# Sixty-four small DRAM-to-DRAM copies, spread one by one through the transfer queue of a windowed-attention and two-MLP kernel

## The chip, the cores and the metric

One core of one Trainium2 chip. The metric is the device time of one execution in microseconds (us); "before" is the median of three executions of the same program. One execution was profiled, and its trace is what all rows below come from. TensorE is PE in the rows (PEld is its load of stationary operands), VectorE is DVE, ScalarE is ACT, GpSimd is POOL, and SP is the engine whose queue issues every transfer of this kernel.

## The reference

Attention over a window of 64 keys, then two MLPs, all in float32; some weights arrive as float64 and are read as 64-bit words.

```
B, H, S, D = 4, 8, 576, 64
scores = q @ k^T / sqrt(D), kept where 0 <= i - j < 64, else -1e9
attn   = exp(scores - max); attn = attn / (sum + 1e-9)
x      = attn @ v, as (2304, 512)
h      = x @ w_in;   x = max(0.01 * h, h) @ w_out        # 512 -> 2048 -> 512
h      = x @ w_in2;  out = (max(h, 0) + log1p(exp(-|h|))) @ w_out2
```

## The kernel before

**Tiles and chunks.** The 2304 tokens are 18 attention tiles of 128, six chunks of 384 for the first MLP. A first-MLP step (c, j) is a *product* (`gemm1_p`, letter G, 12 matmuls of 384 columns into a PSUM tile `ph`), an ACT activation `g` (`gemm1_a`, letter P, line 634), a rounded copy `gh` (letter Q, line 640), the remainder `gl` on DVE (letter R, line 646), and the second product (`gemm2`, letter H, 12 matmuls into four PSUM tiles `o`). Two PSUM buffers hold `ph`, so a new G waits until the P of the second last G has been read.

**The order.** Everything up to about 130 us stands in `HEAD`, a list written out by hand: a letter and a number for each piece, one after another. `ordered` chains the pieces on each engine, so that each engine's order is the list's. After `HEAD` a loop over `steps` does the rest, two slots to a step; what attention needs is put into slots by `attention_slots`.

**The weights of the first MLP.** 32 blocks of 512 KB, keyed by j and by 0 (w_in) or 1 (w_out); the text calls them 9_1, 10_0 and so on. Letter l loads one (`load_w`, lines 147 and 152) into one of three buffers `wraw`; a and b narrow it (ACT line 161, then DVE lines 166 and 168), c and d split it into two halves (ACT or DVE line 466, DVE line 246). A load needs the buffer of the load three before it, which is free when that block's line 168 has read it. The numbers behind l, a, b, c, d in `HEAD` are 2j for j_0 and 2j + 1 for j_1.

**Queries and keys by blocks.** Tiles 0 to 5 are turned on PE. From tile 6 on DVE turns them in 32 by 32 blocks, for which q and k must lie block by block in DRAM: `lay_out(b, parts)` copies batch b of q and k there in 32 small copies (line 405, runs of 128 bytes). Batch 1 takes 32 copies of 48 KB, batch 2 takes 32 of 72 KB. `load_blocks` (line 418) then loads one tile's q and k blocks, `tile_u` (lines 893 and 894) turns them on DVE. All copies and loads stand in SP's one queue, in program order.

Before the change the copies are issued four at a time, ahead of a G:

```python
relay = {5 + n: (lay_out, first, range(n * PARTS // 8, (n + 1) * PARTS // 8)) for n in range(8)}
relay |= {14 + n: (lay_out, first + 1, range(n * PARTS // 8, (n + 1) * PARTS // 8)) for n in range(8)}
```

where the number is the count of G's begun, and three G's can follow each other closely in the list.

**The attention results of tile t** go out to DRAM (`cross`, line 933, `turned`) and come back in four copies (`back`, line 937) before PE multiplies them with v (line 913).

Of the kernel before, what the change touches and what calls it, by code (L numbers as in the profile page):

```python
# [21 lines left out]
def tile_window_attention_two_mlps(  # L22
# [75 lines left out]
    PARTS = 2 * NP * (P // TB)  # L98
# [177 lines left out]
    def keep_places():  # L276


        kept["64"] = [sb.tile([P, DM], I64, tag="raw64", bufs=3, name=f"kept64_{n}") for n in range(3)]

    def keep_more():
        kept["cv"] = cv.rearrange("p n x -> p (n x)")
        part = sb.tile([P, 3, DM], F32, tag="part", bufs=1, name="kept_part")
        kept["part"] = part.rearrange("p n x -> p (n x)")
        kept["hi"] = [[kept[nm][:, 2 * DM :] for nm in ("part", "cv")]]
# [3 lines left out]
    def keep_last():  # L289
        kept["hi"].append([pair[:, n].rearrange("p a b -> p (a b)") for n in range(2)])  # L290
# [654 lines left out]
    def attention_slots(c):  # L945
        at = {}
        put = lambda n, *todo: at.setdefault(n, []).extend(todo)
        for n in range(TPC):
            t = c * TPC + n
            s, d = SLOTS.get(c, LATER)[n]  # L950
            two = ((t, 0), (t, 1))
            put(s - 6, (att_ah, (t,)))
            put(s - 3 - (t == BY_DVE + 1), (tile_u, (t,)))
            put(s - 2 - (t == BY_DVE + 1), (att_aq, (t, "")))
            put(s, (tile_bp, (t,)), *((att_bm, (g, t)) for g in two), *((att_bn, (g,)) for g in two))
            put(s + 1, (att_be, (two[0],)), (att_bs, (two[0],)), (att_bx, (two[0],)), (att_be, (two[1],)))
            put(s + 2, *((f, (two[1],)) for f in (att_bs, att_bx)))
            if t == BY_DVE:
                put(s - 8, (load_qk, (t,)))
                put(s - 2, (load_v, (t,)))  # L960
                put(s + 1, (load_qk, (t + 1,)))
                put(s + 7, (load_qk, (t + 2,)))
            elif t == BY_DVE + 2:
                put(s + 1, (load_qk, (t + 1,)), (load_qk, (t + 2,)))
            elif THIRDS <= t + 1 < NT // P:
                put(s + 1, (load_qk, (t + 1,)))
            put(s + 3, *((turn, (g,)) for g in two), (cross, (t,)))
            put(s + 7, (back, (t,)))
            put(d, (tile_d, (t,)))
            if t + 1 < NT // P:  # L970
                put(d + 1, (load_v, (t + 1,)))
        return at
# [30 lines left out]
        d20 a24 P13 d26 P12 b24 a28 c24v G15 c22 d22 Q13 b28 R13 H14 l25 a25 b25 d24 G18 Q11 Q10 l30 H13  # L1003
        c25 R10 d25 R11 l27 H10 l29 c28v a27 P15 G19 d28 Q12 b27 a29 P18 Q15 a30 b30 H11 R15 b29 c27v
        c29v l23 R12 d29 l31 G20 P20 H12 a23 Q20 H15 c30v d30 b23 a31 b31 R20 P19 d27 c23v G9 Q18 G21
        R18 P9 P21 d23 G22 Q9 R9 H9 c31v Q21 R21 d31 G23 H20 P22 Q19 P23 H21 R19 H18 Q23 Q22 H19 R23 R22
    """.split()
    place = {item.rstrip("vg"): n for n, item in enumerate(HEAD)}
    first_of = {kind: min(place[x] for x in place if x[0] == kind) for kind in "GH"}
# [19 lines left out]
    queues = {}  # L1029
# [3 lines left out]
    def ordered(queues, f, *a, only=None):  # L1033

        seen = len(traced)
        f(*a)
        new = traced[seen:]
        for ins in new:
            if only is not None and ins.engine != only:
                continue  # L1040
            before = queues.get(ins.engine)
            if before is not None:
                tc.add_manual_dep(
                    ins, before.name,
                    mybir.DependencyInfo(mybir.DependencyClass.NoSync, mybir.DependencyReason.DATA),
                    reason="head",
                )
            queues[ins.engine] = ins

    first = BY_DVE * P // S  # L1050
    relay = {5 + n: (lay_out, first, range(n * PARTS // 8, (n + 1) * PARTS // 8)) for n in range(8)}
    relay |= {14 + n: (lay_out, first + 1, range(n * PARTS // 8, (n + 1) * PARTS // 8)) for n in range(8)}

    at_slot = {}

    def plan():
        for n, (c, j, s, e, nxt) in enumerate(steps):
            if s and nxt is not None:
                for i, todo in attention_slots(nxt).items():
                    at_slot.setdefault(2 * (n - CUT - NF) + i, []).extend(todo)  # L1060

    def slot_before(todo, run):
        for f, a in todo:
            if f is tile_bp:
                run(f, *a)
            elif f is tile_d:
                run(tile_dp, a[0], ((a[0], 0), (a[0], 1)))

    def slot_after(todo, run):
        for f, a in todo:  # L1070
            if f is tile_d:
                x = x_of(a[0] // TPC)
                run(att_dh, a[0], "", x[0])
                run(att_dl, a[0], *x)
            elif f is not tile_bp:
                run(f, *a)
# [3 lines left out]
    def rest():  # L1080
        while waiting:
            slot_after(waiting.pop(0), lambda f, *a: ordered(queues, f, *a))

    def slots_until(n):
        rest()
        for i in sorted(i for i in at_slot if i <= n):
            rest()
            todo = at_slot.pop(i)
            slot_before(todo, lambda f, *a: ordered(queues, f, *a))
            waiting.append(todo)  # L1090

    plan()
    begun = 0

    for item in HEAD:
        name = item.rstrip("vg")
        kind = name.rstrip("0123456789")
        n = int(name[len(kind) :])

        held.pop(next((ps for ps, f in READ.items() if f == kind), "") + f"_{n}", None)  # L1100
        if kind == "G":
            if not begun:
                att_tags[:] = ["att"]
            if begun in relay:
                f, *a = relay[begun]
                ordered(queues, f, *a)
            if begun == CUT + NF - AHEAD:
                keep_places()
            slots_until(2 * (begun - CUT - NF))
            begun += 1  # L1110
        if kind == "H":
            slots_until(2 * (begun - 1 - CUT - NF) + 1)
        if kind in pieces_by:
            ordered(queues, pieces_by[kind], n, item[len(name) :])
        else:
            ordered(queues, pieces[kind], n)
        if kind == "P":
            rest()

    def later(f, *a, lag=LAG2):  # L1120

        with tc.issue_after(behind[-lag][0]), tc.issue_after(behind[-lag][1]):
            return f(*a)
# [14 lines left out]
    def ticks(c, j, u):  # L1138
        return int((c > 2 or c == 2 and j >= SKEW) and "end" not in kept)
# [8 lines left out]
    for n, (c, j, s, e, nxt) in enumerate(steps):  # L1148
        if n < CUT + NF:
            continue  # L1150
        if s and c == 2:
            keep_more()
        if s and c == NC - 1:
            keep_last()
        run = lambda f, *a: ordered(queues, f, *a)
        for u in range(2):
            todo = at_slot.get(2 * (n - CUT - NF) + u, ())
            run(save_x2)
            slot_before(todo, run)
            if u == 0:  # L1160
                run(gemm1_p, c, j)
            else:
                run(gemm1_a, c, j)
                run(gemm1_h, c, j)
            slot_after(todo, run)
            if u == 1:
                run(gemm1_l, c, j)
            for _ in range(ticks(c, j, u)):
                run(next, keeper, None)
        if c == 0 and j >= NF - 4:  # L1170
            run(lay_out, 3, range(4 * (j + 4 - NF), 4 * (j + 5 - NF)))
        if c == 2 and 4 <= j < 12:
            run(lay_out, 3, range(8 + 2 * j, 10 + 2 * j))
        if c == NC - 1:
            for f, *a in prepare.get(j, ()):
                run(f, *a)
        if c == 2 and j == 0:
            run(next, keeper)
        if n >= SKEW:
            run(gemm2, *steps[n - SKEW][:4])  # L1180
            run(finish, *steps[n - SKEW][:4])
# [21 lines left out]
    for p in range(2, NPR):  # L1203
        n = last_of[p - 2] if p < NPR - 1 else 8
# [59 lines left out]
    queues = {}  # L1264
# [44 lines left out]
```

## Time and profile before

| | us |
|---|---|
| median of three executions (844.61 to 847.05) | 846.98 |
| the profiled execution | 846.16 |
| its span in the trace | 844.3 |
| PE busy in the span | 821.6 |
| DVE, ACT, POOL busy | 621.0, 428.7, 209.8 |

The profiled execution's time is 1.9 us more than its span. A row of the timeline gives start and length, the engine, the line, what is written and read, and in brackets how long the engine had been idle and what released it.

### The profile page before, as it was taken

What the parts mean: (1) busy time and instruction counts of PE and PEld (TensorE: products, weight loads), DVE (VectorE), ACT (ScalarE), POOL (GpSimd) and SP (SyncE); (2) the same over time, 40 slices, a digit from 0 to 9 for tenths busy, and PEclk for the clock granted to TensorE, in tenths of its full rate; (3) what the DMA queues carried; (4) which work ended last, traced back from release to release, by engine and by line L of the source; (5) the groups of instructions that cost most, each with busy time, mean ns of one, the idle gap of its engine ahead of it and who ended that gap; (6) DMA issues with size and microseconds to landing.
All of it is one profiled execution on the core that took longest, in us unless ns stands there. A gap on an engine that the chain in (4) does not pass through costs nothing.

```text
span 844.3 us, 16526 instructions
## 1 busy us (share of the span) xinstructions
PE 821.6 (97%) x6072; PEld 804.3 (95%) x6072; DVE 621.0 (74%) x1158; ACT 428.7 (51%) x975; POOL 209.8 (25%) x262
## 2 busy tenths in 40 slices
PE   6899799999999999999999999999999999999997
PEld 4799799999999999999999999999999999999997
DVE  6996586525655555555457699999989998989895
ACT  6965354434445544454456555566634444445342
POOL 3211001102332322333126414645511600000000
PEclk9999999999999999999999999999999999999999
DMA  9987886475999879887596544444568884343422
GB/s 226 241 215 205 189 204 145 110 181 170 238 251 260 247 207 262 248 234 195 178 269 174 174 157 144 155 158 150 178 234 271 273 285 151 101 150 101 137 74 91
DMA packets 229201, 161.13 MB, mean 191 GB/s; under 512 B 105728, under 2 KB 198016, under 8 KB 229120
## 3 DMA queue, kind: packets, MB, share of 16 engines
q1 hardware_dynamic: 229120, 160.08, 66.5%
q8 instruction: 48, 0.79, 0.4%
q14 instruction: 33, 0.27, 0.1%
HBM read 105.51 MB, written 60.82 MB: 197 GB/s over the span
## 4 chain that ended last, share of the span: by engine, by line
PE 88%; ACT 3%; DVE 3%; DMA 2%; SPq 2%; issue 1%; POOL 0%; DVEq 0%; ACTq 0%; POOLq 0%
PE ph L614 7%; PE f L858 7%; PE f L850 7%; PE f L857 7%; PE ph L616 7%; PE ph L615 7%; PE o L614 7%; PE p L614 7%; PE p L616 7%; PE p L615 7%; PE o L615 7%; PE o L616 7%; PE po L913 2%; PE ps L489 2%; ACT sm L524 1%; SPq L405 1%
## 5 line engine op out<-in xcount | busy, mean ns | idle before, releaser
L614 PE MATMUL ph<-xh,w 128*128 128x384 f32 x384 | 131.1, 341 | 6.4 <-ACT g L634 6.4
L614 PE MATMUL o<-gh,w 128*128 128x384 f32 x384 | 130.6, 340 | 0.0
L615 PE MATMUL o<-gl,w 128*128 128x384 f32 x384 | 129.1, 336 | 0.4 <-DVE gl L646 0.4
L616 PE MATMUL ph<-xh,w 128*128 128x384 f32 x384 | 129.2, 336 | 0.0
L615 PE MATMUL ph<-xl,w 128*128 128x384 f32 x384 | 129.1, 336 | 0.0
L646 DVE TENSOR_TENSOR gl<-g,gh 128x384 fp32r<-128x384 f32 x96 | 58.6, 612 | 90.4 <-ACT gh L640 90.4
L616 PE MATMUL o<-gh,w 128*128 128x384 f32 x360 | 120.7, 335 | 0.0
L634 ACT ACTIVATE g<-ph 128x384 f32<-128x384 f32 x96 | 46.7, 488 | 142.0 <-PE ph L616 138.7
L537 POOL TENSOR_TENSOR sm<-sm,sums 128x512 f32<-128x512 f32 x36 | 39.4, 1095 | 220.7 <-DVE sums L533 151.6
L614 PEld LDWEIGHTS ph<-xh,w 128*128 128x128 f32 x384 | 72.4, 188 | 8.9 <-ACT g L634 7.3
L614 PEld LDWEIGHTS o<-gh,w 128*128 128x128 f32 x384 | 72.6, 189 | 1.7 <-issue 1.2
L615 PEld LDWEIGHTS o<-gl,w 128*128 128x128 f32 x384 | 72.7, 189 | 0.9 <-DVE gl L646 0.9
L615 PEld LDWEIGHTS ph<-xl,w 128*128 128x128 f32 x384 | 72.6, 189 | 0.0
L616 PEld LDWEIGHTS ph<-xh,w 128*128 128x128 f32 x384 | 72.7, 189 | 0.0
L858 PE MATMUL f<-wq,a 128*128 128x256 f32 x252 | 71.4, 283 | 0.0
L850 PE MATMUL f<-wq,a 128*128 128x256 f32 x252 | 71.3, 283 | 0.0
L857 PE MATMUL f<-wq,a 128*128 128x256 f32 x252 | 71.3, 283 | 0.0
L616 PEld LDWEIGHTS o<-gh,w 128*128 128x128 f32 x360 | 68.1, 189 | 0.0
L524 ACT ACTIVATE sm<-sm,nm 128x128 f32<-128x128 f32 x144 | 55.9, 392 | 10.1 <-DVE nm L513 10.1
L640 ACT CAST gh<-g 128x384 fp32r<-128x384 f32 x96 | 49.1, 512 | 9.3 <-PE o L616 6.9
L858 PEld LDWEIGHTS f<-wq,a 128*128 128x128 f32 x252 | 48.4, 192 | 0.2 <-DVE a L807 0.2
L850 PEld LDWEIGHTS f<-wq,a 128*128 128x128 f32 x252 | 48.4, 192 | 0.0
(317 smaller groups left out, 2182.3 us busy)
## 6 DMA issues: line engine op xcount, KB each, us to landing
in<-hd SPq DMA_DIRECT2D x32, 512.0 KB, 4.9
wraw<-in_moe_w_in_dram SPq DMA_DIRECT2D x16, 512.0 KB, 4.8
wraw<-in_moe_w_out_dram SPq DMA_DIRECT2D x16, 512.0 KB, 4.8
kept<-in_moe_w_in_dram SPq DMA_DIRECT2D x16, 512.0 KB, 5.7
kept<-in_moe_w_out_dram SPq DMA_DIRECT2D x16, 512.0 KB, 5.0
hd<-kept SPq DMA_DIRECT2D x19, 384.0 KB, 2.6
hd<-cv SPq DMA_DIRECT2D x15, 384.0 KB, 2.4
turned<-pair SPq DMA_DIRECT2D x11, 512.0 KB, 3.0
```

The source lines that it names most:

```text
L489: nc.tensor.matmul(ps[h][o, p, :], qT[r, p, o], kT[t][r, p, w0 : w0 + P], start=True, stop=True,)
L524: nc.scalar.activation(sm[:, p, :], sm[:, p, :], AF.Exp, bias=nm[:, p : p + 1], accum_out=sums[:, p : p + 1],)
L537: nc.gpsimd.tensor_tensor(sm, sm, sums.unsqueeze(2).to_broadcast([P, NP, P]), ALU.mult)
L614: nc.tensor.matmul(ps, wh, xh, start=start, stop=False)
L615: nc.tensor.matmul(ps, wh, xl, start=False, stop=False)
L616: nc.tensor.matmul(ps, wl, xh, start=False, stop=stop)
L634: nc.scalar.activation(g, ph, AF.Prelu, alpha=0.01)
L640: a = nc.scalar.copy(gh, g)
L646: b = nc.vector.tensor_tensor(gl, g, gh.bitcast(F32), ALU.subtract)
L850: j = nc.tensor.matmul(ps, gh, wh, start=first and u == 0, stop=False, skip_group_check=True)
L857: nc.tensor.matmul(ps, gh, wl, start=False, stop=False, skip_group_check=True)
L858: j = nc.tensor.matmul(ps, gl, wh, start=False, stop=end, skip_group_check=True)
```

## The change

Each copy becomes an item of a list, and one goes out behind every G and every H of `HEAD`, and behind every weight load l as long as copies of batch 1 remain; it starts when five G's have begun. Copies that are left after `HEAD` go three to a step of the loop. The loads of the blocks of tiles 9 and 10 move six slots later, and in `HEAD` the activation of one product (P22) and the copy of another (Q19) change places.

```diff
@@ attention_slots
             elif t == BY_DVE + 2:
-                put(s + 1, (load_qk, (t + 1,)), (load_qk, (t + 2,)))
+                put(s + 7, (load_qk, (t + 1,)), (load_qk, (t + 2,)))
@@ HEAD
-        R18 P9 P21 d23 G22 Q9 R9 H9 c31v Q21 R21 d31 G23 H20 P22 Q19 P23 H21 R19 H18 Q23 Q22 H19 R23 R22
+        R18 P9 P21 d23 G22 Q9 R9 H9 c31v Q21 R21 d31 G23 H20 Q19 P22 P23 H21 R19 H18 Q23 Q22 H19 R23 R22
@@
-    relay = {5 + n: (lay_out, first, range(n * PARTS // 8, (n + 1) * PARTS // 8)) for n in range(8)}
-    relay |= {14 + n: (lay_out, first + 1, range(n * PARTS // 8, (n + 1) * PARTS // 8)) for n in range(8)}
+    relay = [(b, n) for b in range(first, first + 2) for n in range(PARTS)]
+
+    def lay_next(count=1):
+        for b, n in relay[:count]:
+            ordered(queues, lay_out, b, range(n, n + 1))
+        del relay[:count]
@@ for item in HEAD: if kind == "G"
-            if begun in relay:
-                f, *a = relay[begun]
-                ordered(queues, f, *a)
@@ for item in HEAD, at its end
+        if kind in "GHl" and begun >= 5 and (kind != "l" or relay[0][0] == first):
+            lay_next()
@@ for n, (c, j, s, e, nxt) in enumerate(steps), after the two slots
+        lay_next(3)
```

The same 64 copies are made, in the same order among themselves; PE, DVE and POOL keep their order in every place, ACT in all but the one pair. What moves is SP's queue. First, around the weight loads 8_1 to 10_0. Before, where the last of twelve line 405 copies in a row stands ahead of 9_1:

```order
L405 DMA kd<-in_k_dram 32x12x32
L152 DMA wraw_9_1_1171<-in_moe_w_out_dram 128x512
L152 DMA wraw_10_1_1178<-in_moe_w_out_dram 128x512
L147 DMA wraw_10_0_1181<-in_moe_w_in_dram 128x4x128
L405 DMA qd<-in_q_dram 32x12x32
```

Now the same stretch, from the copy ahead of 8_1 to the one behind 10_0:

```order
L405 DMA qd<-in_q_dram 32x12x32
L152 DMA wraw_8_1_1103<-in_moe_w_out_dram 128x512
L405 DMA kd<-in_k_dram 32x12x32
L405 DMA qd<-in_q_dram 32x12x32
L405 DMA kd<-in_k_dram 32x12x32
L405 DMA qd<-in_q_dram 32x12x32
L152 DMA wraw_9_1_1168<-in_moe_w_out_dram 128x512
L405 DMA kd<-in_k_dram 32x12x32
L152 DMA wraw_10_1_1176<-in_moe_w_out_dram 128x512
L405 DMA qd<-in_q_dram 32x12x32
L147 DMA wraw_10_0_1180<-in_moe_w_in_dram 128x4x128
L405 DMA kd<-in_k_dram 32x12x32
```

Eight of the twelve copies that stood between 8_1 and 9_1 are gone from there; three stand ahead of 8_1, which had none between it and 7_1.

Second, around 14_0 and 12_0, still SP; here the names in brackets are what a row waits for, DMAHW0 to DMAHW7 being the eight semaphores that the transfers use in turn. Before:

```order
L147 DMA wraw_14_0_1321<-in_moe_w_in_dram 128x4x128 [waits DMAHW6_49,DVE_49,Activation_49]
L405 DMA qd<-in_q_dram 32x18x32 [waits DMAHW7_49]
L405 DMA kd<-in_k_dram 32x18x32 [waits DMAHW0_49]
L405 DMA qd<-in_q_dram 32x18x32 [waits DMAHW1_49]
L405 DMA kd<-in_k_dram 32x18x32 [waits DMAHW2_49]
L418 DMA qblocks_1328<-qd 128x4x128 [waits DMAHW3_49]
L418 DMA kblocks_1330<-kd 128x4x128 [waits DMAHW4_49,Pool_49]
L147 DMA wraw_12_0_1373<-in_moe_w_in_dram 128x4x128 [waits DMAHW5_49,DVE_49,Activation_49]
```

Now:

```order
L147 DMA wraw_13_0_1294<-in_moe_w_in_dram 128x4x128 [waits DMAHW7_49,DVE_49,Activation_49]
L405 DMA qd<-in_q_dram 32x12x32 [waits DMAHW0_49]
L405 DMA kd<-in_k_dram 32x12x32 [waits DMAHW1_49]
L147 DMA wraw_14_0_1317<-in_moe_w_in_dram 128x4x128 [waits DMAHW2_49,DVE_49,Activation_49]
L418 DMA qblocks_1320<-qd 128x4x128 [waits DMAHW5_49,DMAHW3_49,DMAHW0_49]
L418 DMA kblocks_1322<-kd 128x4x128 [waits DMAHW4_49,DMAHW6_49,DMAHW1_49,Pool_49]
L405 DMA qd<-in_q_dram 32x18x32
L405 DMA kd<-in_k_dram 32x18x32
L405 DMA qd<-in_q_dram 32x18x32 [waits DMAHW7_49]
L147 DMA wraw_12_0_1368<-in_moe_w_in_dram 128x4x128 [waits DVE_49,Activation_49]
```

The last two copies of batch 1 (the rows with 32x12x32) now stand right ahead of 14_0, and `qblocks`, which reads what they write, waits for them by DMAHW0. Before, eleven rows of weight loads and copies lay between.

Third, later in SP's queue, where the loop issues the loads of tiles 9 and 10 (`kept`). Now they stand behind the v loads of tile 8 and four copies of batch 3:

```order
L372 DMA vs_2143<-in_v_dram 128x8x64
L372 DMA vn_2145<-in_v_dram 128x8x64
L405 DMA qd<-in_q_dram 32x18x32
L405 DMA kd<-in_k_dram 32x18x32
L405 DMA qd<-in_q_dram 32x18x32
L405 DMA kd<-in_k_dram 32x18x32
L418 DMA kept_1_1663<-qd 128x4x128
L418 DMA kept_1_1663<-kd 128x4x128
L418 DMA kept_0_1662<-qd 128x4x128
L418 DMA kept_0_1662<-kd 128x4x128
```

Before, these four `kept` rows stood ahead of the line 933 copy and of those two v loads.

## Rows read from the trace of the kernel before

**Rows 1.** The page, busy time of each engine: us, share, instructions.

```profile
PE 821.6 (97%) x6072; PEld 804.3 (95%) x6072; DVE 621.0 (74%) x1158; ACT 428.7 (51%) x975; POOL 209.8 (25%) x262
```

**Rows 2.** Stretches: length, busy PE, PEld, DVE, ACT, POOL, clock, DMA share, GB/s.

```profile
80.00:85.00 5.00, 5.00 (x31) 5.00 (x30) 1.18 (x2) 1.27 (x3) 0.00 (x0) 1.00 0.99 320
...
105.00:110.00 5.00, 3.36 (x13) 3.36 (x14) 3.51 (x7) 3.36 (x7) 0.00 (x0) 0.78 0.89 183
140.00:160.00 20.00, 19.60 (x163) 18.54 (x162) 9.95 (x20) 8.94 (x28) 2.08 (x2) 1.00 0.35 81
```

**Rows 3.** Timeline, ACT and PE, 87 to 90 us.

```profile
87.62 0.66 ACT L161 ACTIVATE cv<-wraw 128x512 f32<-128x512 f32 x1
88.91 0.51 ACT L634 ACTIVATE g<-ph 128x384 f32<-128x384 f32 x1
89.47 0.44 PE L614 MATMUL ph<-xh,w 128*128 128x384 f32 x1 [3.55 <-ACT g L634]
```

**Rows 4.** Timeline of SP, 68 to 80 us; twelve L405 rows from 70.13 to 78.68.

```profile
68.63 1.45 SPq L152 DMA_DIRECT2D wraw<-in_moe_w_out_dram  x2
70.13 0.56 SPq L405 DMA_DIRECT2D qd<-in_q_dram  x1
...
78.68 1.02 SPq L152 DMA_DIRECT2D wraw<-in_moe_w_out_dram  x2
79.80 0.38 SPq L147 DMA_DIRECT2D wraw<-in_moe_w_in_dram  x1
```

**Rows 5.** Timeline of DVE: line 168 reads 7_1, then 8_1.

```profile
73.99 0.75 DVE L168 SCALAR_TENSOR_TENSOR cv<-wraw,cv 128x512 uint16<-128x512 uint32 x1
...
76.82 0.75 DVE L168 SCALAR_TENSOR_TENSOR cv<-wraw,cv 128x512 uint16<-128x512 uint32 x1
```

**Rows 6.** Chain of work: weight loads 6_0, 10_1, 12_0 from issue to landing.

```profile
48.40 3.66 DMA wraw<-in_moe_w_in_dram
...
79.33 6.21 DMA wraw<-in_moe_w_out_dram
...
100.02 5.45 DMA wraw<-in_moe_w_in_dram
```

**Rows 7.** Timeline of PEld: eleven loads from 90.65, twelve from 94.11.

```profile
90.65 0.27 PEld L615 LDWEIGHTS ph<-xl,w 128*128 128x128 f32 x1
...
94.11 0.19 PEld L614 LDWEIGHTS o<-gh,w 128*128 128x128 f32 x1
...
96.22 0.19 PEld L614 LDWEIGHTS ph<-xh,w 128*128 128x128 f32 x1
```

**Rows 8.** Timeline, SP, ACT and PEld, 88 to 107 us (13_0, 14_0, blocks, wait).

```profile
88.02 2.92 SPq L147 DMA_DIRECT2D wraw<-in_moe_w_in_dram  x2
...
94.91 0.56 SPq L147 DMA_DIRECT2D wraw<-in_moe_w_in_dram  x1
...
98.51 0.72 SPq L418 DMA_DIRECT2D qblocks<-qd  x1
...
105.55 0.66 ACT L161 ACTIVATE cv<-wraw 128x512 f32<-128x512 f32 x1 [5.86 <-DMA wraw<-in_moe_w_in_dram]
...
106.64 0.19 PEld L614 LDWEIGHTS ph<-xh,w 128*128 128x128 f32 x1 [3.12 <-ACT g L634]
```

**Rows 9.** Line 405 from 70 to 78.6 us, then from 90.9 to 98 us.

```profile
DMA to landing us min/median/max: 2.3/2.7/4.9
...
DMA to landing us min/median/max: 3.4/4.1/4.8
```

**Rows 10.** Timeline of SP and DVE, 138 to 184 us.

```profile
138.05 2.61 SPq L937 DMA_DIRECT2D pair<-turned  x4
155.05 0.33 SPq L933 DMA_DIRECT2D turned<-cv  x1
...
171.63 1.81 SPq L372 DMA_DIRECT2D vn<-in_v_dram  x1
...
183.80 0.70 DVE L893 STREAM_TRANSPOSE qT<-kept 128x512 f32<-128x512 f32 x1
```

## Prediction

> **What bounds the kernel now.** I read the page's busy times first: PE is busy 821.6 of 844.3 us [rows 1], so time can only come from the some 23 us in which it is not, or in which its clock is low. Going through the stretches I looked for a PE column below the length or a clock below 1.00. Behind 60 us there are two such places, near 86 to 94 and near 104 to 111 us, and hardly another: from 140 to 160 us 0.4 us are idle, at clock 1.00 [rows 2]. The reader should see there that ACT and DVE are far from full, so neither is too slow; something reaches them late.
>
> The first place: PE idles 3.55 us up to 89.47, released by ACT's g at 88.91 (product 9 of chunk 1), which had to stand behind the narrowing of block 10_0 at 87.62 in ACT's order [rows 3]. That block and the two before it were loaded at 78.68 to 79.80, behind twelve copies of line 405, issued one after another from 70.13: (78.68 - 70.13) / 12 = 0.71 us a copy [rows 4]. These copies, and no transfer's bytes, held the queue. 10_1 took 6.21 us to land, at 85.54 [rows 6]. The second place: PEld idles 3.12 us up to 106.64, behind the narrowing of 12_0 at 105.55, whose load was issued at 100.02 and landed after 5.45 us [rows 6, 8]. After each wait PE runs at the lower of its two clock levels for a while: from 90.65 to 94.11 eleven loads take 3.46 us, afterwards twelve take 2.11 us, or 0.176 each [rows 7]. So a slow stretch costs 3.46 - 11 x 0.176 = 1.5 us. The stretch from 105 to 110 with clock 0.78 is the second one [rows 2].
>
> **First wait.** 7_1 goes at 68.63 as before. Three copies now stand ahead of 8_1: 68.63 + 0.38 (a weight load's own issue, as at 79.80) + 3 x 0.71 = 71.1; it was the second of the pair that ends at 70.08, so it left at about 69.7 and is 1.4 later [rows 4]. Four copies behind it bring 9_1 to 71.1 + 0.38 + 2.84 = 74.3, 4.3 earlier than 78.68. Its buffer is free (9_0 is read ahead of 7_1, thus before 73.99). One more copy: 10_1 at 75.4, against 79.3; its buffer is free at 73.99 + 0.75 = 74.74. One more: 10_0 could go at 76.5, but needs the buffer of 8_1, read until 77.57 before, and up to 1.4 later now [rows 5]. So 10_0 leaves between 77.6 and 79.0, centre 78.3, instead of 79.80.
>
> Landing has no row for this new order; the bounds are 3.66 us (6_0) and 6.21 us (10_1, half a microsecond behind another weight load) [rows 6]. 10_0 now follows a weight load by some 3 us with one copy between, half way: 4.9. It lands at 83.2, bounds 81.3 and 85.2. From the narrowing to g 1.29 us passed and from g to PE 0.56 [rows 3]; with 0.1 to start, PE could go on at 85.15, bounds 83.2 and 87.15. It comes there at 89.47 - 3.55 = 85.92. The wait shrinks from 3.55 to between 0 and 1.2; I leave 0.25. The slow stretch should go with it, since idling of 0.4 us within 140 to 160 us left the clock at 1.00 [rows 2]. Gain 3.3 + 1.5 = 4.8 us.
>
> The slow stretch lost 1.5 us by its rows [rows 7]. The Trainium skill (TensorE: Matmul & The Clock Gate, Terms) puts the penalty at the throttled time times one less the clock's share, here half of 3.46 us, an estimate of 1.7 us; by it the sum below would be 0.2 us lower.
>
> **Second wait.** PE now arrives 4.8 us earlier; the question is whether 12_0 does. g moves from 88.91 to about 84.6 (83.2 + 0.1 + 1.29). 13_0, second of the two loads that end at 90.94, left at about 90.6, 1.7 behind g [rows 3, 8]: now 86.3. The last two copies of batch 1 follow it, the second at 86.3 + 0.38 + 0.71 = 87.4, and 14_0 behind them at 88.1, or 6.0 behind g as before (94.91 against 88.91), 90.6 at the latest. Then comes what the change adds: `qblocks` has to wait until these two copies have landed, 3.4 to 4.8 us after issue [rows 9]. They follow a weight load directly, as those did that took longest, so I take 4.8: `qblocks` at 92.2, earliest 90.8, against 98.51. Everything behind it in SP's queue waits too: the k blocks, three copies and 12_0. From `qblocks` to 12_0 it was 1.51 us (98.51 to 100.02) and is 2.1 more by the three copies: 12_0 at 95.8, earliest 95.1 - 0.7 = 94.4. It is 4.2 earlier (at best 5.6) while PE is 4.8 earlier, so with 5.45 us to land the second wait grows by 0.6; landing as fast as 3.66 would take 1.8 off, 6.21 would add 0.8. I take +0.5, and the second slow stretch stays.
>
> **The rest.** The other moved copies cost nothing: SP has nothing to issue between 140.66 and 155.05 [rows 10], where six of them (4.3 us) go; PE, DVE and POOL keep their order. The pair swapped on ACT is one of 0.5 us rows (0.51 at 88.91, [rows 3]) where PE is full: between -0.5 and +0.5, taken as 0. Tiles 9 and 10 load later: the v loads ahead end at 173.44 before; four loads (2.8) leave from ahead of them, four copies (2.8) enter, and four more copies stand behind: tile 9's pair goes at 176.3 and 177.0 and, with the 6.21 us of [rows 6], has landed by 183.2, while DVE turns tile 9 at 183.80 [rows 10]. All these instants move together with PE. Without that cover of 0.6 us DVE's `gl`, queued behind the turn, would be late, and then PE.
>
> **Sum.** -3.3 - 1.5 + 0.5 = -4.3 us on the profiled execution's 846.16: **841.9 us**. That execution lies 0.8 below the median of 846.98.
>
> **Rivals.**
> Both waits end. If the copies land in 2.3 us as the quickest did [rows 9], `qblocks` goes at 89.7 or when 14_0 has gone, and if 12_0 then lands in 3.66 us, at some 97, PE, arriving at about 98.9, loses little. Then 3.55 + 3.1 + 2 x 1.5 less a rest of 0.5: 837.0. Speaking against it: 14_0's own buffer, and 5.45 us on the row.
>
> Transfers bind instead of the queue. From 80 to 85 us the DMA share is 0.99 at 320 GB/s [rows 2]. If mixed copies and loads land late, 10_0 at 86.0 or later, 2.0 to 3.5 us of the first wait and its slow stretch stay: gain 0 to 1.6, about 845. Against it: the twelve copies in a row landed in 2.7 us at the median [rows 9], so they drained as they were issued. That the change does nothing, since buffers hold the loads, would give the same 846; the two buffers were free 4 us before their loads left [rows 4, 5].
> The Trainium skill (DMA: Bandwidth & Descriptors, Bandwidth) speaks for this rival: it calls transfers under 64 KB descriptor-dominated and has 0.95 us for one of 64 KB. Taken for our 48 KB, an estimate, the four copies ahead of 9_1 would need 3.8 us, and 9_1, 10_1 and 10_0 would land 1 to 2 us later than I say, with the time near 844. The twelve that were issued every 0.71 us and landed without piling up [rows 4, 9] bear it out little.
>
> `qblocks` as a worse plug. At SP's place behind 14_0 everything stands until batch 1 has landed. If 10_0 still comes late, 13_0 leaves at 90.6, the copies at 91.7, and if they take 6.21 us to land, as 10_1 did [rows 6], `qblocks` goes at 97.9 and 12_0 3.6 later at 101.5: 1.5 us later than before, so 847.7, and 848 to 850 with 0.8 us more for its own landing and a longer slow stretch. It decides from 12_0 leaving after 100.02 with the first wait still there, or after about 104.8 with it gone.
>
> **Chances.** Forecast 0.57, both waits end 0.14, transfers bind or nothing changes 0.21, worse plug 0.08. The forecast's own range is 840 to 844, from a first wait left between 0 and 1.2 (then perhaps with its slow stretch) and the second between -1.3 and +1.4. The range for 8 in 10 reaches half way into the first rival and to the middle of the second: 838.0 to 845.6. Within 0.3% (2.5 us, about what a measurement of this kernel can tell) of the median means 844.4 to 849.5. Faster: nearly all of the forecast, the first rival and a third of the second, 0.75; same 0.19; slower 0.06.
>
> **What would show it.** SP's rows: 9_1 at about 74, 10_0 at 78 to 79, `qblocks` at about 92 and 12_0 at about 96, with a gap on SP ahead of `qblocks`. PE: no wait above 0.5 us near 86, clock 1.00 from 85 to 95, one wait near 99 to 103 of about 3.5 us and one slow stretch behind it. ACT's pass over 10_0 at about 83. Wrong would be: 10_0 landing after 86, a PE wait behind tile 9 after 175, or a wait near 99 that is gone or above 5 us.

## The result and the profile after

| | median (lowest to highest), us | ratio to before, 95% interval |
|---|---|---|
| before, beside it | 847.01 (844.61 to 848.09) | |
| changed | 838.63 (838.38 to 839.98) | 0.9908 [0.9885, 0.9932] |

The change makes the kernel 0.9% faster, and the time lies in the range. The profiled execution took 838.38 us with a span of 836.6, so its span is 7.7 us shorter than that of before, where the forecast took 4.3 off. The direction and the end of the first wait were right; the size came out at nearly twice the sum, and the following views show from which terms.

The page's row of busy times, which answers to [rows 1]: PE's work shrinks by 3.8 us, though the same 6072 matmuls are made.

```profile
PE 817.8 (98%) x6072; PEld 801.1 (96%) x6072; DVE 620.9 (74%) x1158; ACT 428.5 (51%) x975; POOL 209.7 (25%) x262
```

The stretches, with the columns of [rows 2]. From 85 to 90, where PE had idled 3.55 us, it is full. From 95 to 105 some 1.7 us are left idle. The clock is 1.00 in all of them, where before 90 to 95 stood at 0.66, as the first of these rows shows, and 105 to 110 at 0.78: neither of the two slow stretches is there any more. Before:

```profile
90.00:95.00 5.00, 5.00 (x21) 5.00 (x20) 3.32 (x6) 1.38 (x3) 0.00 (x0) 0.66 0.85 226
```

and after:

```profile
80.00:85.00 5.00, 5.00 (x31) 5.00 (x30) 3.57 (x8) 5.00 (x11) 0.00 (x0) 1.00 0.82 194
85.00:90.00 5.00, 5.00 (x31) 5.00 (x30) 3.63 (x8) 1.98 (x5) 0.00 (x0) 1.00 0.85 221
90.00:95.00 5.00, 5.00 (x31) 5.00 (x30) 3.75 (x8) 2.27 (x4) 0.00 (x0) 1.00 0.76 222
95.00:100.00 5.00, 3.60 (x21) 3.28 (x19) 0.96 (x3) 0.76 (x2) 0.00 (x0) 1.00 0.99 212
100.00:105.00 5.00, 4.66 (x27) 4.67 (x28) 4.71 (x9) 3.42 (x8) 0.00 (x0) 1.00 0.78 220
105.00:110.00 5.00, 5.00 (x30) 5.00 (x29) 4.59 (x9) 1.48 (x3) 0.00 (x0) 1.00 1.17 298
```

SP's timeline, cut to 9_1, 10_0, 14_0, the two block loads and 12_0. It answers to [rows 4] and [rows 8]. 9_1 left at 74.85 instead of 78.68, 10_0 at 78.40 instead of 79.80, 12_0 at 94.90 instead of 100.02.

```profile
74.85 0.54 SPq L152 DMA_DIRECT2D wraw<-in_moe_w_out_dram  x1
...
78.40 0.38 SPq L147 DMA_DIRECT2D wraw<-in_moe_w_in_dram  x1
...
88.40 0.37 SPq L147 DMA_DIRECT2D wraw<-in_moe_w_in_dram  x1
90.34 0.58 SPq L418 DMA_DIRECT2D qblocks<-qd  x1
91.90 0.57 SPq L418 DMA_DIRECT2D kblocks<-kd  x1
94.90 0.57 SPq L147 DMA_DIRECT2D wraw<-in_moe_w_in_dram  x1
```

The timeline of ACT and PE at the two places. ACT narrows 10_0 at 83.27 (before 87.62, [rows 3]) and makes product 9's `g` at 84.57 (88.91), ahead of PE, which doesn't wait. 9_1 and 10_1 are narrowed one after the other at 80.70, with no wait on a transfer, and ACT is busy without a gap from 80 to 85 (the row of stretches above). At the second place ACT sits idle until 12_0 lands, at 99.24, and PE waits 1.74 us.

```profile
80.70 1.23 ACT L161 ACTIVATE cv<-wraw 128x512 f32<-128x512 f32 x2
...
83.27 0.67 ACT L161 ACTIVATE cv<-wraw 128x512 f32<-128x512 f32 x1
84.57 0.52 ACT L634 ACTIVATE g<-ph 128x384 f32<-128x384 f32 x1
99.24 0.66 ACT L161 ACTIVATE cv<-wraw 128x512 f32<-128x512 f32 x1 [4.79 <-DMA wraw<-in_moe_w_in_dram]
100.34 0.44 PE L614 MATMUL ph<-xh,w 128*128 128x384 f32 x1 [1.74 <-ACT g L634]
```

Before, ACT had stood still for 10_1 until 85.62, and 10_0 itself needed 7.1 us from issue to landing. ACT's timeline, and the view of 10_0's load issued at 79.80:

```profile
85.62 0.66 ACT L161 ACTIVATE cv<-wraw 128x512 f32<-128x512 f32 x1 [2.13 <-DMA wraw<-in_moe_w_out_dram]
DMA to landing us min/median/max: 7.1/7.1/7.1
```

After, the view of 10_0's load issued at 78.40:

```profile
DMA to landing us min/median/max: 4.1/4.1/4.1
```

To see where the 7.7 us came from, the same five instructions of PE's order are put side by side, since PE's order hasn't changed: the first matmul of a product, one of a second product that comes behind the first wait, and the scores of three attention tiles. PE's timeline before:

```profile
81.60 0.33 PE L614 MATMUL ph<-xh,w 128*128 128x384 f32 x1
...
99.51 0.33 PE L614 MATMUL o<-gh,w 128*128 128x384 f32 x1
...
118.84 1.10 PE L489 MATMUL ps<-kT,qbd 64*64 64x128 f32 x32
...
158.83 1.10 PE L489 MATMUL ps<-kT,qbd 64*64 64x128 f32 x32
...
256.29 1.10 PE L489 MATMUL ps<-kT,qbd 64*64 64x128 f32 x32
```

and after:

```profile
81.80 0.33 PE L614 MATMUL ph<-xh,w 128*128 128x384 f32 x1
...
94.28 0.33 PE L614 MATMUL o<-gh,w 128*128 128x384 f32 x1
...
110.96 1.10 PE L489 MATMUL ps<-kT,qbd 64*64 64x128 f32 x32
...
150.21 1.10 PE L489 MATMUL ps<-kT,qbd 64*64 64x128 f32 x32
...
248.48 1.10 PE L489 MATMUL ps<-kT,qbd 64*64 64x128 f32 x32
```

After stands at +0.20, -5.23, -7.88, -8.62 and -7.81 us, and the span at -7.7. So in these two traces the first place gave 5.43, the second 2.65, the stretch up to 158 us another 0.74, and between 158 and 256 us 0.81 was given back.

### The profile page after: what moved, and what is told of

Same layout as the page of the kernel before. It is cut to its first block, busy times and chain, and to the rows that moved or that the text cites. A ratio compares the mean times of both kernels' runs of the same rounds, so it can differ in the third digit from the quotient of the medians.

```text
span 836.6 us, 16527 instructions
## 1 busy us (share of the span) xinstructions
PE 817.8 (98%) x6072; PEld 801.1 (96%) x6072; DVE 620.9 (74%) x1158; ACT 428.5 (51%) x975; POOL 209.7 (25%) x262
## 4 chain that ended last, share of the span: by engine, by line
PE 85%; DVE 7%; DMA 3%; ACT 2%; SPq 2%; issue 1%; POOL 0%; DVEq 0%; POOLq 0%; ACTq 0%
PE o L614 8%; PE ph L614 8%; PE o L615 7%; PE o L616 7%; PE ph L615 7%; PE ph L616 7%; PE p L614 7%; PE p L615 7%; PE p L616 7%; PE f L858 5%; PE f L857 5%; PE f L850 5%; PE po L913 2%; DVE a L807 2%; PE ps L489 2%
## 5 line engine op out<-in xcount | busy, mean ns | idle before, releaser
L646 DVE TENSOR_TENSOR gl<-g,gh 128x384 fp32r<-128x384 f32 x96 | 56.9, 593 | 90.0 <-ACT gh L640 90.0
```

The lines of the kernel that those rows point to most:

```text
L646: b = nc.vector.tensor_tensor(gl, g, gh.bitcast(F32), ALU.subtract)
```

## The experiments

All were run with the kernel before on the same chip; its median was 845.78, 845.74 and 845.97 us in the three groups. They stand here by what they test.

**One batch alone.** The first of two halves of the change: batch 1 goes singly, batch 2 stays in fours, nothing else is touched.

```diff
-    relay = {5 + n: (lay_out, first, range(n * PARTS // 8, (n + 1) * PARTS // 8)) for n in range(8)}
+    singles = list(range(PARTS))
...
+        if kind in "GHl" and begun >= 5 and singles:
+            ordered(queues, lay_out, first, [singles.pop(0)])
```

> Batch 1's copies go singly, batch 2's stay in fours ahead of a product, the loads of tiles 9 and 10 stay where they were before. Theory (each wait is set by the copies in SP's queue ahead of its own weight load): 9_1 leaves near 75 and 10_0 near 78, so the first PE wait and its slow stretch are gone as in the changed kernel; but ten batch-2 copies now stand between 13_0 and 12_0, so 12_0 leaves 0.7 to 1.5 us after the changed kernel's 94.9 and the second PE wait is 2.4 to 3.3 us instead of 1.74, with or without a slow stretch. Tile 8's results come back in time, 0.7 us less there. About 839.5 to 841. Rival (the single copies of batch 2 carry half of the gain by themselves, through a lighter load on the transfers): second wait as long as before or longer, 842 to 843.

Measured 841.99 us (840.61 to 845.03), 0.9962 [0.9947, 0.9978]. The first wait is gone and the second is there in full: 12_0, still behind two blocks of four copies, leaves at 96.15 and PE waits 3.27 us, after which a stretch at clock 0.70 follows. SP's and PE's timeline, and then the stretch:

```profile
94.65 0.72 SPq L418 DMA_DIRECT2D qblocks<-qd  x1
...
96.15 0.56 SPq L147 DMA_DIRECT2D wraw<-in_moe_w_in_dram  x1
...
101.82 0.51 PE L614 MATMUL ph<-xh,w 128*128 128x384 f32 x1 [3.27 <-ACT g L634]
```

```profile
100.00:105.00 5.00, 3.18 (x10) 3.18 (x11) 3.31 (x7) 3.46 (x7) 0.00 (x0) 0.70 0.99 206
```

This looks like the case that the forecast described for the whole change: first wait gone, second a little longer than the 2.80 us of before on PE, its slow stretch kept. The wait is in the range of the theory, but the time isn't; it fits the rival's 842 to 843, and without single copies of batch 2 the second wait doesn't shrink. It isn't a lighter load on the transfers, as the rival had it, that makes most of the difference: 12_0 reached ACT 4.58 us after its issue here and 4.34 in the changed kernel, while it left 1.25 us later.

The other half: batch 1 stays in fours, batch 2 goes singly behind every G and H from the fifteenth G on, three to a step after the list, with the two smaller edits of the change.

```diff
+    fours = {5 + n: (lay_out, first, range(n * PARTS // 8, (n + 1) * PARTS // 8)) for n in range(8)}
+    relay = [(first + 1, n) for n in range(PARTS)]
...
+        if kind in "GH" and begun >= 15:
+            lay_next()
```

> The other half: batch 1's copies stay in fours, batch 2's go singly behind a product, the rest three to a step, tiles 9 and 10 load six slots later. Theory: the twelve copies in a row are still ahead of 9_1, which leaves near 78.7, and the first PE wait stays at 3.3 to 3.8 us with its slow stretch of 1.5 us; the second shrinks to 0.5 to 1.5 us, because 12_0 then leaves as soon as 11_0 has been read, near 98 instead of 100.0, and the blocks of tile 6 wait for nothing. No second slow stretch. About 842 to 843.5, which together with the other half's gain makes more than the whole change. Rival (the first wait comes from weights that are slow to land, with the copies as a whole to blame): the first wait is under 2 us here as well, and the time near 840.

Measured 841.66 us (840.22 to 843.1), 0.9954 [0.994, 0.9969]. The halves' gains, 0.38 and 0.46%, add to 0.84%, near the 0.92% of the whole. But the first wait came out smaller than the 3.3 to 3.8 expected, 2.45 us, and with no slow stretch behind it, and the second longer, 1.71 us for 0.5 to 1.5; the time lies just below the 842 to 843.5 of the theory. PE's timeline, and then the stretches:

```profile
88.73 0.44 PE L614 MATMUL ph<-xh,w 128*128 128x384 f32 x1 [2.45 <-ACT g L634]
103.22 0.45 PE L614 MATMUL ph<-xh,w 128*128 128x384 f32 x1 [1.71 <-ACT g L634]
```

```profile
85.00:90.00 5.00, 2.55 (x15) 2.23 (x14) 4.39 (x9) 3.68 (x8) 0.00 (x0) 1.00 0.63 108
90.00:95.00 5.00, 5.00 (x31) 5.00 (x30) 2.78 (x6) 3.03 (x6) 0.00 (x0) 1.00 0.99 303
```

**The plug at `qblocks`.** The forecast said that `qblocks` has to stand in SP's queue until the last two copies of batch 1 have landed. In the trace of the changed kernel 14_0 is issued at 88.40, `qblocks` at 90.34 and the load of the k blocks at 91.90; its chain of work names the last of these copies:

```profile
87.26 4.58 DMA kd<-in_k_dram
```

The edit lays the remaining copies of batch 1 out ahead of an earlier load (11_0), so that nothing just issued is waited for:

```diff
+        while item == "l22" and relay[0][0] == first:
+            lay_next()
```

> The changed kernel with the last four copies of batch 1 ahead of 11_0, so that the blocks of tile 6 need not wait for copies that have just been issued. Theory (what is left of the second wait is the plug: SP stands 2.1 us at tile 6's blocks until batch 1 has landed): no gap on SP there, 12_0 leaves at 92 to 93.2 instead of 94.90, the PE wait of 1.74 us falls to 0 to 0.4. About 1.5 us less than the changed kernel, 836.8 to 837.5. Rival (12_0 is held by its buffer or by landing): PE wait still above 1.2 us, the time within 0.5 us of the changed kernel's.

Measured 835.95 us (834.99 to 836.73), 0.9883 [0.9867, 0.9899]. The gap is gone, 12_0 leaves 2.0 us earlier than in the changed kernel, and no wait of PE is left near 100. The time is 0.9 below the 836.8 expected at best; the wait near 178 that the next experiment is about isn't in this trace either. SP's timeline:

```profile
87.96 0.37 SPq L147 DMA_DIRECT2D wraw<-in_moe_w_in_dram  x1
88.43 0.58 SPq L418 DMA_DIRECT2D qblocks<-qd  x1
89.11 0.58 SPq L418 DMA_DIRECT2D kblocks<-kd  x1
92.88 0.66 SPq L147 DMA_DIRECT2D wraw<-in_moe_w_in_dram  x1
```

**Tile 8's results.** In the changed kernel's trace PE waits 0.73 us for tile 8's `pair`, a wait that before didn't have. SP's timeline of that kernel, and PE's:

```profile
167.83 0.63 SPq L418 DMA_DIRECT2D kept<-qd  x1
...
170.53 3.78 SPq L937 DMA_DIRECT2D pair<-turned  x4
...
178.50 0.69 PE L913 MATMUL po<-pair,vs 128*64 128x64 f32 x16 [0.73 <-DMA pair<-turned]
```

The four copies back stand behind the four loads for tiles 9 and 10 (2.7 us). One slot more puts these loads behind them:

```diff
-                put(s + 7, (load_qk, (t + 1,)), (load_qk, (t + 2,)))
+                put(s + 8, (load_qk, (t + 1,)), (load_qk, (t + 2,)))
```

> The changed kernel with the loads of tiles 9 and 10 one slot later, behind the four copies that bring tile 8's attention results back. Theory (PE's wait of 0.7 us, PEld's 1.0, at 178 us in the changed kernel is for these copies, queued behind the four loads): that wait is gone, no wait at tile 9 in its place, time 0.7 us less, 837.7 to 838.2 by the span. Rival (the copies themselves are slow to land or leave late because DVE is late): the wait stays at 0.5 us or more.

Measured 836.9 us (836.23 to 837.65), 0.9896 [0.9882, 0.991]. The wait at 178 is gone in its trace; the one near 100 is 1.05 us there, though nothing ahead of 160 us was changed. The time is 0.8 below the lowest expected, so not all of it can come from the loads. Nor is the cause of the wait shown by this run: the unaltered changed kernel, profiled again below, has no wait at 178 either.

**12_0 earlier, in the changed kernel.** The loads of 12_0 (l24) and 14_0 (l28) change places in the list, first together with the edit before, then alone.

```diff
-        ... G12 b22 l28 a26 G13 H17 H16 b26 l24 R14 c26 c20v
+        ... G12 b22 l24 a26 G13 H17 H16 b26 l28 R14 c26 c20v
```

> The changed kernel with the loads of tiles 9 and 10 one slot later (behind tile 8's own copies back) and with the loads of 12_0 and 14_0 exchanged in the list. Theory (the second wait is as long as 12_0 leaves late, behind the blocks and three copies): 12_0 now leaves at about 88 instead of 94.2, ACT narrows it at about 94 instead of 98.6, and the wait of 1.1 us that was left near 100 is gone; 14_0 leaves at about 94 and is needed later, so no new wait of over 0.3 us. The time is about 1 us below the 836.9 of the kernel with only the loads later: 835.5 to 836.2. Rival (the transfers around 90 to 100 us bind, whatever their order): a wait of about 1 us stays there, on 12_0 or on 14_0, and the time is 836.5 to 837.5.

Measured 835.45 us (835.01 to 836.78), 0.9889 [0.987, 0.9907], 1.45 below the kernel with the loads later alone, where about 1 was expected.

> The changed kernel with the loads of 12_0 and 14_0 exchanged and nothing else, so with the loads of tiles 9 and 10 where the change has them. Theory (two waits of their own): the wait near 100 is gone, that of some 0.7 us on tile 8's copies back near 178 stays; 836.5 to 837.2, between the changed kernel and the 835.45 with both edits. Rival (the wait near 178 depends on how SP's queue stands by then and goes too, as it went where the copies were laid out earlier): 835 to 836.

Measured 835.14 us (834.44 to 838.47), 0.9883 [0.9857, 0.9908]. In both the wait near 100 is gone. ACT's timeline of the second: 12_0 is narrowed at 95.16 with no wait on a transfer, and what now comes by transfer, 14_0 at 98.56, is not late for PE.

```profile
95.16 0.68 ACT L161 ACTIVATE cv<-wraw 128x512 f32<-128x512 f32 x1 [0.88 <-DVE w L246]
```

The edit alone was expected between 836.5 and 837.2; it came out lower. The wait at 178 was not in its trace, as the rival said; another wait of 0.55 us on `pair` stood at 250.00.

**12_0 earlier, in the kernel before.** The same exchange, nothing else.

> The kernel before with the loads of 12_0 and 14_0 exchanged in the list, nothing else. Theory (the second wait hangs on 12_0's place in the queue alone): the first wait stays at about 3.5 us with its slow stretch, 12_0 leaves at about 95 instead of 100, the second wait of 2.8 us on the matmul row and its slow stretch of 1.5 us are gone: 4.3 us less, 841 to 842.5. Rival (14_0, now late, is needed as soon): a wait of 1.5 us or more stays near 105 and the time is 843.5 to 846.

Measured 845.29 us (842.57 to 846.4), 0.9992 [0.998, 1.0005]: no difference that can be measured. The second wait did go (PE isn't idle from 100 to 110), but one of 3.17 us with a slow stretch of its own came at 117.61. The rival was right that a wait remains, though neither its place nor its block: the one behind it is 13_1. PE's timeline, and then the stretches:

```profile
88.36 0.69 PE L614 MATMUL ph<-xh,w 128*128 128x384 f32 x1 [2.43 <-ACT g L634]
...
117.61 0.44 PE L614 MATMUL ph<-xh,w 128*128 128x384 f32 x1 [3.17 <-ACT g L634]
```

```profile
85.00:90.00 5.00, 2.57 (x11) 2.25 (x10) 4.75 (x10) 3.26 (x8) 0.00 (x0) 0.80 0.56 104
90.00:95.00 5.00, 5.00 (x27) 5.00 (x26) 1.81 (x4) 2.09 (x5) 0.00 (x0) 0.86 1.00 257
115.00:120.00 5.00, 2.39 (x10) 2.39 (x11) 2.76 (x5) 3.37 (x7) 0.00 (x0) 0.87 0.51 89
```

and the two weight loads on its chain of work:

```profile
102.38 4.58 DMA wraw<-in_moe_w_out_dram
...
109.25 7.25 DMA wraw<-in_moe_w_out_dram
```

SP issues without a gap there: 12_1 leaves at 102.38 behind four copies, and 13_1 at 109.25 behind four more, 15_0 and two v loads. With single copies the exchange gained 2.6 us by the medians of the last group (837.78, below, to 835.14; both intervals overlap), and 1.45 together with the later loads; with blocks of four the next load in the queue was late in its stead.

**The swap of P22 and Q19** undone in the changed kernel:

```diff
-        ... G23 H20 Q19 P22 P23 H21 R19 H18 Q23 Q22 H19 R23 R22
+        ... G23 H20 P22 Q19 P23 H21 R19 H18 Q23 Q22 H19 R23 R22
```

> The changed kernel with the activation of product 22 ahead of the copy of block 19 again, as in the kernel before; nothing else. Theory (it sits where PE is full, and changes places of 0.5 us rows): within 0.5 us of the changed kernel, 838.1 to 839.1, with PE as busy from 140 to 160 us as there. Rival (the swap is what removed the 0.40 us wait of PE at 149 us): that wait is back and the time is 0.4 us longer, 838.8 to 839.2.

Measured 837.68 us (837.27 to 838.13), 0.9913 [0.9895, 0.993]. The view of what PE waited for between 100 and 200 us has the 0.4 us of before again:

```profile
PE o L615 <- DVE gl L646: 0.4, 1, 0.4
```

In the traces with the old order (before, batch 1 alone, 12_0 earlier in the kernel before, this one) the wait is there, in those with the new order it isn't. So the swap takes 0.4 us of wait away, as the rival said; the times themselves don't resolve it, and 837.68 lies below what both expected.

**The changed kernel and the best of the others, again**, on one chip, together with the exchange alone above.

> The changed kernel itself, unaltered, for a comparison on the same chip with the next two and with the kernel whose swap was undone (837.68). Theory (its time is that of its waits, 1.7 us near 100 and 0.7 near 178): 837.5 to 839.0, with both waits again. Rival (the waits near 178 and 100 come and go between executions of the same program): 836 to 837.5, with one of the two gone from the profile.

Measured 837.78 us (836.2 to 839.54), 0.9907 [0.9885, 0.9929]. PE's waits from 60 to 300 us in its trace are this one row, so tile 8's wait was not there, as the rival said it might be, and the second was 1.17 us:

```profile
PE ph L614 <- ACT g L634: 1.2, 1, 1.2
```

> The kernel with the last copies of batch 1 laid out earlier, once more, beside the changed kernel on the same chip, since adding the later loads of tiles 9 and 10 to it gave 837.2 and not the 835.5 to 836.0 that were expected. Theory (laying out earlier takes the wait near 100 away): 1.5 to 2.7 us below the changed kernel of this call, 835.5 to 836.5, no PE wait above 0.5 us between 85 and 110. Rival (the 835.95 was one chip's or one call's luck): within 1 us of the changed kernel.

Measured 836.35 us (835.27 to 837.68), 0.9893 [0.9872, 0.9914], 1.4 us below the changed kernel, with the wait near 100 down to 0.61 us and one of 0.41 us on a tile's `pair` at 250.60. It is just short of the 1.5 expected, and both intervals overlap. The gap at the block loads is gone again, but 12_0 left at 94.29, no earlier than in the changed kernel of this group (94.31): the loads and copies ahead of it, from the k blocks on, took 1.09, 0.91, 1.00 and 1.22 us to issue.

**Both later edits together**, the early copies of batch 1 and the loads of tiles 9 and 10 a slot later:

> The changed kernel with the last copies of batch 1 ahead of the load that stands some items earlier in the list, and with the loads of tiles 9 and 10 one slot later, both edits that each took 1.7 to 2.7 us off by themselves. Theory (two separate costs, the plug at the block loads and the copies back of tile 8): the kernel with only the first edit already had no wait of PE behind 60 us but one of 0.4 us, so the second adds 0 to 0.4 us: 835.5 to 836.0. Rival (each removes a wait of its own, 1.1 and 0.7 us, and they add): 834.0 to 835.0, and the kernel with the first edit alone would have to show a wait near 178 us, which it doesn't.

Measured 837.2 us (836.22 to 837.57), 0.9903 [0.9885, 0.9921]: no better than either edit alone, and 1.2 above the top of what was expected. In its trace PE waits 0.54 us near 100 and 0.95 at 251.38 for another tile's `pair`:

```profile
PE po L913 <- DMA pair<-turned: 0.9, 1, 0.9
```

Such waits of 0.4 to 0.95 us on tiles' results between 170 and 260 us came in four of the traces with the new order and not in others, one at 178.50 and three from 250.00 to 251.38. What makes them come or go was not isolated.

## Why the prediction came out as it did

**First wait: gone as forecast, in part by luck, and the gain mis-sized.** The loads left where the prediction said (9_1 at 74.85 for 74.3, 10_0 at 78.40 for 78.3), and `g` came at 84.57 for 84.6. The step between them is right by luck. The sum lets 10_0 land 4.9 us after its issue and has ACT narrow it at once. It landed after 4.1 us, at 82.5, and ACT, busy without a gap, came to it only at 83.27: what ACT had to do first set that instant. Before, too, ACT was held up by 10_1, until 85.62, and read 10_0 in its turn. The landing also changed, which the prediction left out. 10_0 needed 7.1 us before, above the sum's bound of 6.21; it took 6.8 and 6.9 us in the two other traces with batch 1 in fours, and 4.0 to 5.1 us in the ten with single copies. So of the 4.4 us by which it landed earlier, 1.4 come from leaving earlier and 3.0 from landing faster.

The rest of 0.25 us that was left in the sum isn't there, and by PE's instants the place gave 5.43 us where the sum had 4.8: the wait's 3.55, and 1.88 for its slow stretch and PE's restart, where 1.5 was taken. The Trainium skill (TensorE: Matmul & The Clock Gate, Terms) gave an estimate of 1.7 us for the stretch; the trace lies within 0.2 us of it, with 1.5 by the weight loads of [rows 7] and 1.88 by the instants.

**The plug: right in kind, smaller than said.** `qblocks` stood behind 14_0 until the copies had landed, with a gap on SP. But it left at 90.34, just below the earliest bound of 90.8, and the one that waited longest was the load behind it, at 91.90 for a copy that landed after 4.58 us. 12_0 left at 94.90, 0.9 earlier than the 95.8 of the sum and inside its bounds. With batch 1 laid out earlier the gap is gone in three traces and the second wait is 0, 0.61 and 0.54 us; in the four traces of the changed order with the gap (the changed kernel twice, the later loads, the swap undone) it is 1.74, 1.17, 1.05 and 1.34. So the early copies shorten the wait. How much of it is the gap is less clear: 12_0 left at 92.88, 94.29 and 93.68 without it and between 94.22 and 94.90 with it.

**Second wait: the step that failed.** "I take +0.5, and the second slow stretch stays." The wait shrank by 1.06 us (2.80 to 1.74 on PE), and the stretch went: 1.58 us more, from the 2.65 between the instants less 1.06. Two sizes did it: 12_0 left 0.9 us earlier than in the sum, and ACT had it 4.34 us after issue (94.90 to 99.24) where 5.45 to landing had been carried over from the row of before [rows 6]. In the second trace of the changed kernel it was 94.31 to 98.60, 4.29. With batch 1 alone ACT had it after 4.58 us too, so the 5.45 was no property of the blocks of four around it. There the wait was 3.27 us, the 2.80 + 0.5 of the sum, but by other terms: 12_0 left at 96.15, 0.35 later than the sum has it, and landed faster. Against that kernel the changed one's wait is 1.53 us shorter, 1.25 of it by 12_0's earlier departure, and the slow stretch is gone with it. That a shorter wait alone takes the stretch away is not shown, as the last section says.

The rival "both waits end" (837.0) had half of this: the stretch went, the wait didn't. The measured 838.63 lies nearer to it than to the forecast of 841.9, and outside the forecast's own 840 to 844. It is inside the range given only because that range reaches half way into the rival; the likeliest value was taken too close to the slow end.

**The swap, taken as 0:** the 0.40 us wait at 149 us went with it; up to 158 us PE gained 0.74, of which the rest was not traced.

**The tail, taken as 0:** the cover was said to hang on tile 9's turn, and a wait of PE behind tile 9 after 175 us was named as a sign of being wrong. What was late at 178 instead was tile 8's copies back, which stand behind the four loads that moved; the prediction followed only the moved ones. It cost 0.73 us of wait (0.81 by the instants) in the profiled execution and nothing in the second, where these copies stood behind the same four loads but took 2.60 us to issue instead of 3.78. So their place in the queue alone doesn't bring the wait.

Put together with the steps' own signs: -5.43 for -4.8, -2.65 for +0.5, -0.74 for 0, +0.81 for 0, some 0.3 us at both ends of the span; -7.7 for -4.3.

**The rivals.** That mixed copies and loads land late didn't come: 9_1, 10_1 and 10_0 landed 4.1, 4.9 and 4.1 us after issue with single copies round them, and ACT waited for none of the three. But the transfers were no bystanders before: the three loads, issued within 1.5 us behind the twelve copies, landed after 4.1, 6.2 and 7.1 us, with a DMA share of 0.99 from 80 to 85 us [rows 2], where the changed kernel has 0.82. The Trainium skill (DMA: Bandwidth & Descriptors, Bandwidth) has 0.95 us for a transfer of 64 KB, for loads issued from GpSimd; the loads 1 to 2 us late and the 844 that the prediction worked out from it didn't come. `qblocks` as a worse plug didn't come, since it needed the first wait to stay.

The median of the second group of the changed kernel, 837.78, lies 0.2 below the range given, the first inside it: the range was set too tight on the fast side.

## What to carry to other kernels

Many small transfers in front of a large one cost the large one their issue time, here 0.7 us for each, and the large ones that then left close behind one another landed up to 3 us later here than with the copies spread; spread the small ones singly, and lay out whatever a load will read some loads ahead, so that the load doesn't stop the queue behind it. When loads move in a queue, list what is issued behind them as well, and when the first of two waits is removed, work out the second anew, with its departure and its landing in the new order. When the engine that needs a load has other work queued, follow that work as well: the load's landing may not be what it waits for. A load brought forward in a queue gives something only if the next one isn't late in its place, as the same exchange showed: nothing with blocks of four, 2.6 us by the medians with single copies.

## What the runs showed of the hardware

A wait's length alone did not decide whether a slow stretch of PE's clock followed. A wait of 2.45 us (batch 2 alone, at 88.73) left the granted clock at 1.00, one of 2.43 us at the same place (12_0 earlier in the kernel before, at 88.36) was followed by stretches at 0.80 and 0.86. Waits of 1.05 to 1.74 us left it at 1.00 in every trace here, those of 2.80, 3.17, 3.27 and 3.55 us brought one each. What separates the two of 2.4 us was not found.

The first wait itself was 3.55 us in the trace of before, and 2.43 and 2.45 in two kernels whose order up to there was the same; 10_1 landed 6.2 us after issue in the first and 4.7 and 4.6 in the other two. So one profiled wait of this kind is uncertain by about a microsecond, and with it the sum that is built on it.
